# Loading batch zero's first keys in fp32 on SyncE, and its second softmax on two-bank tiles

## Chip, cores and metric

One core of a Trainium2 chip. The metric is the device time of one execution in microseconds (us), the median of several. On one core there is no second die to compare with.

## The reference, cut to what matters

```python
batch, n_heads, seq, head_dim = (8, 8, 576, 64);  n_pack = 32
def sm_attn(qq, kk, vv):                 # scale = 1/8
    s = scale * np.matmul(qq, kk.transpose(0, 1, 3, 2));  s = s - np.max(s, axis=-1, keepdims=True)
    a = np.exp(s);  a = a / (np.sum(a, axis=-1, keepdims=True) + 1e-09)
    return np.matmul(a, vv)
p_packed = sm_attn(p, k, v)              # 32 packed tokens a head look at 576 tokens
out = sm_attn(q, p_packed, p_packed)     # 576 tokens look at the 32
x = out.transpose(0, 2, 1, 3).reshape(8 * 576, 512)
h = x @ w_in                             # 512 -> 2048
y = (np.maximum(h, 0) ** 2) @ w_out      # 2048 -> 512
```

## The kernel before

The kernel merges the second attention and w_in: M = p_packed times w_in, then F1 = attention weights times M, squared, and F2 times w_out. Its steps for a batch: X (expand p into pT_bd), Tk and Tq (transposes of keys and queries on VectorE, DVE), S1 (p times keys), PV (times values), XT (pq_bd), M, S2 and N (second softmax), F1, F2. A planner simulates the engines while the program is built and so fixes the order of instructions on every engine; the durations in it are only its guesses.

All loads but the first p go through GpSimd's queue (POOL), which casts fp32 to bf16 on the way; I call it the casting queue.

```python
def dma_kq(self, name, qd):                      # one tile: 4 heads of keys or queries, 288 KB in bf16
    t = ... qkv.tile([P, JT * D], BF16, tag="kqb")
    nc.gpsimd.dma_start(t, src[self.b, qd * QH:(qd + 1) * QH].rearrange("h (a j) d -> (h a) (j d)", j=JT))
# [cut]
def ps_s(self, hf):                              # PSUM tile of the second softmax
    if hf is None:                               # whole tokens (all batches but 0): two banks, pool shared with F1
        ps = ps_h.tile([P, 2, 512], F32, name="ps_s", tag="h");  keep_clock(ps[:, 0, :256])
        return ps[:, :, :HALF]
    ps = ps_att.tile([P, 512], F32, name="ps_a", tag="a")   # batch 0, half of the tokens: one bank, shared with M
    keep_clock(ps[:, :256])                      # matmuls on zeros in a planned gap of TensorE
    return ps[:, :HALF].unsqueeze(1)
# [cut] order of the loads:
# p of batches 0, 1 (ACT queue) | k, k, v x4, q x2 of batch 0, w_in x2, q x2 (second halves), w_in x6, w_out x2,
# k, k, v x4, q, q of batch 1, w_out x6, k, k of batch 2, p of batches 2 to 7, v x4, q, q of batch 2, batch 3 ...
```

The softmax here doesn't subtract the row's maximum and nothing guards it: scores larger than these inputs give would overflow.

## Time and profile before

Median 252.97 us (252.92 to 253.29). The profiled execution spans 252.1 us; a second profile of the same kernel, taken later, spans 251.3 us, and the times of the timed runs belong to spans of about 251.3 us, so that the first profile is a slow one of its kind.

| what | before |
|---|---|
| TensorE (PE) busy from 60 to 250 us | 188.0 of 190 us |
| rate of the casting queue from 10 to 44 us | 202 GB/s landed (204 in the second profile) |
| first S1 / PV / S2 / F1 of batch 0 | 6.9 / 11.85 / 17.56 / 23.06 us |
| TensorE's waits from 23 to 66 us | 1.6 us |

From the page of the kernel before, three rows of 40 slices of 6.3 us: busy tenths of PE, mean busy tenths of the DMA engines, GB/s moved.

```profile
...
PE   4887989999999999999999999999999999999993
...
DMA  6999999999999972589111111110122013122233
GB/s 112 184 206 202 205 207 208 197 241 219 216 213 231 219 138 48 86 143 176 42 47 39 42 46 42 42 44 13 41 52 64 10 43 79 42 73 72 70 79 83
...
```

TensorE is nearly full from the seventh slice on, but the DMA engines are full from the second to the fourteenth, at 184 to 241 GB/s: work can't run ahead of its load. (TensorE's busy time up to 25 us is in good part clock-keeping matmuls: 11.8 us of them in this profile, none later.)

The chain that ended last, from its first 70 us: start, length, what.

```profile
...
3.02 6.76 DMA v_r<-in_v_dram
...
18.42 10.68 DMA k_b<-in_k_dram
...
29.38 8.45 DMA w_out_b<-in_moe_w_out_dram
...
38.12 11.37 DMA p_b<-in_p_dram
...
54.20 8.53 DMA v_r<-in_v_dram
...
```

It runs through one load after the other. The timeline (start, length, engine, line, operation, output and inputs, shapes, count; in brackets the idle time before and what ended it):

```profile
...
6.01 0.84 DVE L455 STREAM_TRANSPOSE kT<-k_b 128x320 f32<-128x320 f32 x2 [1.21 <-DMA k_b<-in_k_dram]
...
6.90 1.04 PE L466 MATMUL ps_a<-pT_bd,kT 128*128 128x128 bf16 x8 [3.32 <-DVE kT L455]
...
11.28 0.49 DVE L352 COPY v_b<-v_r 128x1280 bf16<-128x1280 bf16 x1 [3.04 <-DMA v_r<-in_v_dram]
...
11.85 0.28 PE L501 MATMUL ps_pp<-e,v_b 128*128 128x64 bf16 x4
...
15.05 0.61 PE L539 MATMUL ps_a<-w_in_b,pp 64*32 64x512 bf16 x8
...
17.56 0.65 PE L566 MATMUL ps_a<-qT,pq_bd 128*128 128x288 bf16 x4
...
23.06 1.14 PE L615 MATMUL ps_h<-a,M 128*128 128x288 bf16 x8
...
```

p has landed at 3.0 us. The keys land at 6.0, when DVE transposes the first, the last values at 11.15, when DVE casts v_b. M (L539, the 64x512 matmuls) comes before S2 (L566, ps_a), and both use the two one-bank tiles, so that S2 follows M's casts; F1 (L615) starts at 23.06 us.

The windows of the first microseconds; the last three columns are granted clock, DMA share and GB/s (this early, the 1.00 of the clock is no reading; see e13 and e14):

```profile
...
core 0: us, PE busy (x) PEld busy (x) DVE busy (x) ACT busy (x) POOL busy (x), PEclk, DMA share, GB/s
...
2.50:3.00 0.50, 0.50 (x5) 0.34 (x3) 0.27 (x1) 0.00 (x0) 0.50 (x1) 1.00 1.05 71
3.00:3.50 0.50, 0.50 (x3) 0.10 (x1) 0.46 (x2) 0.00 (x0) 0.50 (x2) 1.00 0.81 69
3.50:4.00 0.50, 0.09 (x1) 0.00 (x0) 0.45 (x3) 0.00 (x0) 0.50 (x2) 1.00 0.87 143
4.00:4.50 0.50, 0.00 (x0) 0.00 (x0) 0.47 (x3) 0.00 (x0) 0.50 (x2) 1.00 0.96 175
...
```

From 2.0 to 2.5 us, at 226 GB/s, p came in as fp32. The casting queue then starts at 70 GB/s and needs until about 4.5 us to reach its steady rate. The two longest groups of TensorE's waits from 23 to 66 us:

```profile
...
engine line waited for: us in total, times, longest us
PE ps_o L671 <- DMA w_out_b<-in_moe_w_out_dram: 0.7, 2, 0.5
PE ps_a L466 <- POOL pT_bd L352: 0.4, 1, 0.4
...
```

### The profile page before, as it was taken

Reading aid. Unit: us, or ns where it says so; the run is one execution under the profiler, and the core shown is the slowest. Engines: PE = TensorE matmul, PEld = TensorE weight load, DVE = VectorE, ACT = ScalarE, POOL = GpSimd, SP = SyncE. Lnnn points to the kernel's source line nnn. Section 1 sums busy time; section 2 is a strip of 40 time slices with the busy share of each in tenths; the row PEclk is TensorE's granted clock in tenths of the full one; section 3 lists DMA queues with packets and bytes.
Section 4 is the critical chain, followed back from the end, with each engine's and each line's share of the span. In section 5 each row is a group of like instructions: output and inputs, shape, how many; then the busy total and the mean of one; then the engine's idle time right before and its main releaser. Section 6 shows DMA issues by size and latency. Waiting matters only on the chain.

```text
span 252.1 us, 4976 instructions
## 1 busy us (share of the span) xinstructions
PE 239.6 (95%) x1935; PEld 143.6 (57%) x1935; DVE 143.5 (57%) x249; ACT 158.4 (63%) x275; POOL 61.7 (24%) x122
## 2 busy tenths in 40 slices
PE   4887989999999999999999999999999999999993
PEld 2765674466645666666456665665555655544453
DVE  5453968688988666895675858855146405400000
ACT  2448786678778777886687767777876853511110
POOL 7696465385655401150100000000000000000000
PEclk9999999999999999999999999999999999999999
DMA  6999999999999972589111111110122013122233
GB/s 112 184 206 202 205 207 208 197 241 219 216 213 231 219 138 48 86 143 176 42 47 39 42 46 42 42 44 13 41 52 64 10 43 79 42 73 72 70 79 83
DMA packets 27159, 28.44 MB, mean 113 GB/s; under 512 B 5760, under 2 KB 18816, under 8 KB 27136
## 3 DMA queue, kind: packets, MB, share of 16 engines
q0 software_dynamic: 19504, 18.55, 46.2%
q1 hardware_dynamic: 6912, 9.32, 13.8%
q10 hardware_dynamic: 720, 0.26, 0.4%
q8 instruction: 15, 0.25, 0.4%
q14 instruction: 8, 0.07, 0.1%
HBM read 37.22 MB, written 9.44 MB: 185 GB/s over the span
## 4 chain that ended last, share of the span: by engine, by line
PE 69%; DMA 20%; POOL 5%; SPq 1%; issue 1%; DVE 1%; ACT 1%; DVEq 0%; ACTq 0%; POOLq 0%
PE ps_o L671 40%; PE ps_h L605 19%; DMA v_r<-in_v_dram 6%; DMA p_b<-in_p_dram 5%; DMA k_b<-in_k_dram 4%; DMA w_out_b<-in_moe_w_out_dram 3%; PE ps_m L539 3%; PE ps_s L566 2%; DMA out_dram<-o_sb 2%; PE ps_a L466 2%; POOL w_in_b L428 2%; SPq L680 1%; PE ps_pp L501 1%; PE ps_s L578 1%; POOL v_r L420 1%
## 5 line engine op out<-in xcount | busy, mean ns | idle before, releaser
L671 PE MATMUL ps_o<-w_out_b,gT 128*128 128x512 bf16 x560 | 143.8, 379 | 1.0 <-DMA w_out_b<-in_moe_w_out_dram 0.7
L634 ACT ACTIVATE r<-ps_h 128x576 bf16<-128x576 f32 x112 | 70.9, 649 | 25.8 <-PE ps_h L605 22.4
L671 PEld LDWEIGHTS <-gT 128*128 128x128 bf16 x560 | 53.6, 98 | 47.6 <-issue 3.6
L605 PE MATMUL ps_h<-a,M 128*128 128x288 bf16 x448 | 71.1, 286 | 0.0
L641 DVE TENSOR_TENSOR gT<-r 128x1152 bf16<-128x1152 bf16 x64 | 47.0, 751 | 24.6 <-ACT r L634 14.3
L605 PEld LDWEIGHTS <-M 128*128 128x128 bf16 x448 | 43.6, 98 | 25.0
L352 DVE COPY o_sb<-ps_o 128x512 f32<-128x512 f32 (+1 forms) x19 | 12.8, 676 | 45.2 <-PE ps_o L651 27.6
L350 ACT COPY o_sb<-ps_o 128x512 f32<-128x512 f32 (+1 forms) x18 | 10.3, 575 | 31.3 <-DMA out_dram<-o_sb 23.0
L352 DVE CAST M<-ps_m 128x1024 bf16<-128x1024 f32 x14 | 17.1, 1224 | 11.6 <-PE ps_m L539 11.6
L449 DVE STREAM_TRANSPOSE qT<-q_b 128x1152 bf16<-128x1152 bf16 (+1 forms) x18 | 21.9, 1232 | 3.2 <-DMA q_b<-in_q_dram 3.1
L420 POOL DMA_DIRECT2D v_r<-in_v_dram x32 | 18.8, 592 | 9.4 <-DVE v_b L352 3.3
L350 ACT CAST M<-ps_m 128x1024 bf16<-128x1024 f32 x14 | 14.2, 1012 | 6.5 <-PE ps_m L539 6.4
L592 DVE SCALAR_TENSOR_TENSOR a<-e,rD,ls 128x576 bf16<-128x576 bf16 (+1 forms) x18 | 13.1, 745 | 4.5 <-ACT ls L586 4.3
L473 ACT ACTIVATE e<-ps_a 128x512 bf16<-128x512 f32 x16 | 8.8, 597 | 9.9 <-PE ps_a L466 9.8
L455 DVE STREAM_TRANSPOSE kT<-k_b 128x320 f32<-128x320 f32 (+1 forms) x32 | 12.9, 449 | 1.8 <-DMA k_b<-in_k_dram 1.8
L352 POOL COPY pT_bd<-pT 32x128 bf16<-32x128 bf16 x28 | 10.0, 358 | 13.9 <-PE ps_a L480 12.4
L573 ACT ACTIVATE e<-ps_s,rD 128x576 bf16<-128x576 f32 x14 | 9.7, 738 | 5.3 <-PE ps_s L566 5.3
L466 PE MATMUL ps_a<-pT_bd,kT 128*128 128x128 bf16 x128 | 9.5, 231 | 3.7 <-DVE kT L455 3.3
L408 POOL DMA_DIRECT2D k_b<-in_k_dram x16 | 8.7, 544 | 15.9 <-DVE kT L455 6.5
L374 PE MATMUL ps_a<-idle_b 128*128 128x256 bf16 x59 | 9.1, 306 | 3.2 <-ACT e L573 1.4
L466 PEld LDWEIGHTS <-kT 128*128 128x128 bf16 x128 | 8.5, 103 | 6.0 <-DVE kT L455 4.0
L374 PEld LDWEIGHTS <-idle_b 128*128 128x128 bf16 x79 | 8.3, 107 | 6.4 <-issue 3.9
(65 smaller groups left out, 197.9 us busy)
## 6 DMA issues: line engine op xcount, KB each, us to landing
out_dram<-o_sb SPq DMA_DIRECT2D x140, 64.0 KB, 1.7
k_b<-in_k_dram POOLq DMA_DIRECT2D x16, 288.0 KB, 8.8
q_b<-in_q_dram POOLq DMA_DIRECT2D x14, 288.0 KB, 8.9
v_r<-in_v_dram POOLq DMA_DIRECT2D x16, 160.0 KB, 8.6
v_r<-in_v_dram POOLq DMA_DIRECT2D x16, 128.0 KB, 8.5
w_in_b<-in_moe_w_in_dram POOLq DMA_DIRECT2D x8, 256.0 KB, 7.7
w_out_b<-in_moe_w_out_dram POOLq DMA_DIRECT2D x8, 256.0 KB, 9.3
q_b<-in_q_dram POOLq DMA_DIRECT2D x4, 144.0 KB, 6.9
```

What stands on the lines that cost most here:

```text
L350: nc.scalar.copy(dst, src)
L352: eng.tensor_copy(dst, src)
L374: nc.tensor.matmul(ps, lhsT=idle_b[:, :P], rhs=idle_b, start=True, stop=True)
L420: nc.gpsimd.dma_start(self.vr[32 * i:32 * i + 32, h0:h1, :n * D], src[:, :, J0[i] * D:(J0[i] + n) * D])
L449: nc.vector.transpose(self.qT[:, qd, :, j0 * 32:j1 * 32].rearrange("p dh (j a) -> p j dh a", a=32), self.t.qb[qd][:, j0 * D:j1 * D].rearra ...
L455: nc.vector.transpose(self.kT[:, qd, :n * P].rearrange("p (g jp a) -> p jp g a", jp=4, a=32)[:, i:i + 2], self.t.kb[qd][:, J0[i] * D:(J0[i ...
L466: nc.tensor.matmul(ps[:, g * P:(g + 1) * P], lhsT=self.kT[:, qd, g * P:(g + 1) * P].bitcast(BF16).rearrange("p (t two) -> p two t", two=2) ...
L592: nc.vector.scalar_tensor_tensor(out=self.a2[:, qd, n0:n1].rearrange("p (c n) -> p c n", n=HALF), in0=self.e2[qd, hf], scalar=self.rD[:, q ...
L605: nc.tensor.matmul(ps[:, c, :HALF], lhsT=a.M[:, qd, fb * FB:(fb + 1) * FB], rhs=a.a2[:, qd, c * HALF:(c + 1) * HALF], start=(qd == 0), sto ...
L634: nc.scalar.activation(dst, src, ACT.Relu)
L641: eng.tensor_tensor(out=gT[:, fb - 1:fb + 1, o:o + S], in0=r, in1=r, op=ALU.mult)
L671: nc.tensor.matmul(po[t], lhsT=gT[:, fb, n0:n0 + P], rhs=w_out_b[:, fb, :], start=(fb == 0), stop=(fb == NFB - 1))
```

## The change

Its intent: key tile 0 of batch 0 is the first thing that the kernel needs. SyncE can load it at once as fp32, in parallel with GpSimd's issues, and ScalarE and VectorE each cast a half. One load less is then in the casting queue. And batch 0's second softmax needs no longer wait for M's tiles. Cut to its core (left out are the planner's durations of other steps, changed by up to 0.08 us, and its start times of the engines, changed by 0.2 to 0.4 us):

```diff
+            def dma_k_f32(self, qd):
+                self.kf = stg.tile([P, JT * D], F32, name="k_f", tag="kf")
+                nc.sync.dma_start(self.kf, k[self.b, qd * QH:(qd + 1) * QH].rearrange(...))
+                self.kb[qd] = qkv.tile([P, JT * D], BF16, name="k_b", tag="kqb")
+            def cast_k(self, qd, i, eng):
+                w = JH * D
+                cast(eng, self.kb[qd][:, i * w:(i + 1) * w], self.kf[:, i * w:(i + 1) * w])
             def ps_s(self, hf):
-                if hf is None:
+                if hf is None or self.b in SPLIT:
                     ps = ps_h.tile([P, 2, 512], F32, name="ps_s", tag="h")
-                    return ps[:, :, :HALF]
+                    return ps[:, :2 if hf is None else 1, :HALF]
-                return [kq("k", 0), kq("k", 1)] + vv(0, 1) + [ ...
+                return [kq("k", 1)] + vv(0, 1) + [ ...
-            return [res[0], res[2], res[1], res[4], res[3], res[6], res[5], res[7]]
+            return [res[0], res[2], res[1], res[3], res[4], res[6], res[5], res[7]]   # S2, S2, N, N of the first halves
+        plan.stream(0, [Step("Lk.0.0", [stage([("SP", 0.45, lambda: L[0].dma_k_f32(0))]), ...
+        plan.stream(5, [Step("Ck.0.0", ...   # the halves on ACT or DVE
```

More of the change, by code (lines that the diff above doesn't have):

```diff
@@ L24 @@
 BDW = 384
+SPLIT = (0,)
 INF = float("inf")
@@ L408, in dma_kq @@
                 nc.gpsimd.dma_start(t, src[self.b, qd * QH:(qd + 1) * QH].rearrange("h (a j) d -> (h a) (j d)", j=JT))
+            def dma_k_f32(self, qd):
+                self.kf = stg.tile([P, JT * D], F32, name="k_f", tag="kf")
+                nc.sync.dma_start(self.kf, k[self.b, qd * QH:(qd + 1) * QH].rearrange("h (a j) d -> (h a) (j d)", j=JT))
+                self.kb[qd] = qkv.tile([P, JT * D], BF16, name="k_b", tag="kqb")
+            def cast_k(self, qd, i, eng):
+                w = JH * D
+                cast(eng, self.kb[qd][:, i * w:(i + 1) * w], self.kf[:, i * w:(i + 1) * w])
             def dma_q_half(self, qd, hf):
@@ L715, in load_steps @@
             if b in SPLIT:
-                return [kq("k", 0), kq("k", 1)] + vv(0, 1) + [
+                return [kq("k", 1)] + vv(0, 1) + [
                     load_step(f"Lq.{b}.{qd}.{hf}", 0.56, 0.78, lambda qd=qd, hf=hf: L[b].dma_q_half(qd, hf), [("kqb", 1)] if hf == 0 else [])
@@ L741, in tr_steps @@
             if nm == "q" and b in SPLIT:
-                return [Step(f"Tq.{b}.{qd}.{hf}", [stage([("DVE", 0.71, lambda qd=qd, hf=hf: T[b].tr_q(qd, hf))])],
+                return [Step(f"Tq.{b}.{qd}.{hf}", [stage([("DVE", 0.78, lambda qd=qd, hf=hf: T[b].tr_q(qd, hf))])],
                              [f"Lq.{b}.{qd}.{hf}"] + old, (), [("kqb", 0, f"Lq.{b}.{qd}.0")] if hf else []) for hf in range(2) for qd in QDS]
             return [Step(f"T{nm}.{b}.{qd}", [stage([("DVE", us, lambda qd=qd: (T[b].tr_k if nm == "k" else T[b].tr_q)(qd))])],
-                         [f"L{nm}.{b}.{qd}"] + old, (), [("kqb", 0, f"L{nm}.{b}.{qd}")]) for qd in QDS]
+                         [f"Ck.0.0" if (nm, b, qd) == ("k", 0, 0) else f"L{nm}.{b}.{qd}"] + old, (),
+                         [("kqb", 0, f"L{nm}.{b}.{qd}")]) for qd in QDS]
         def s1_steps(b):
@@ L773, in m_steps @@
                              [stage([("PE", 0.66, lambda c=c: T[b].m(c))]),
-                              stage(*[[("ACT", 1.05, lambda c=c, e=e: T[b].m_out(c, e, A)),
-                                       ("DVE", 1.15, lambda c=c, e=e: T[b].m_out(c, e, V))] for e in QDS])],
+                              stage(*[[("ACT", 1.01, lambda c=c, e=e: T[b].m_out(c, e, A)),
+                                       ("DVE", 1.23, lambda c=c, e=e: T[b].m_out(c, e, V))] for e in QDS])],
                              [f"XT.{b}/1.0"] + [f"LWI.{2 * c + j}.{i}" for i in range(2) for j in range(2)], [("h", 2)], [("h", 1, None)])
@@ L790, in s2_steps @@
             wide = b in WIDE
-            pool, m = ("h", 2) if wide else ("a", 1)
+            pool, m = "h" if wide or b in SPLIT else "a", 2 if wide else 1
             for qd, hf in halves(b):
@@ L801, in s2_steps @@
                                  stage([("ACT", 0.65 if wide else 0.43, lambda qd=qd, hf=hf: T[b].n_inv(qd, hf))]),
-                                 stage([("DVE", 0.75 if wide else 0.46, lambda qd=qd, hf=hf: T[b].n_mul(qd, hf))])],
+                                 stage([("DVE", 0.82 if wide else 0.52, lambda qd=qd, hf=hf: T[b].n_mul(qd, hf))])],
                                 [f"S2.{b}.{qd}.{hf}"], [(pool, 1), ("ls", 1)],
@@ L897, in kernel_impl @@
         NB_ACTQ = -1
-        SPLIT = (0,)
         WIDE = tuple(b for b in range(B) if b not in SPLIT)
@@ L902, in kernel_impl @@
         setup()
-        plan.base.update(DVE=2.5, POOL=0.8, ACT=0.5, SP=0.3, DMA=1.2, PE=3.6)
+        plan.base.update(DVE=2.7, POOL=1.2, ACT=0.75, SP=0.7, DMA=1.2, PE=3.6)
         plan.stream(0, [pload(0, 2)])
@@ L908, in kernel_impl @@
         plan.stream(0, ld)
+        plan.stream(0, [Step("Lk.0.0", [stage([("SP", 0.45, lambda: L[0].dma_k_f32(0))]), stage([("-", 0.75, lambda: None)]),
+                                        stage([("DMA", 1.5, lambda: None)])], (), [("kqb", 1)], (), lag=0.7)])
+        plan.stream(5, [Step("Ck.0.0", [stage([("-", 0.0, lambda: None)]),
+                                        stage(*[[("ACT", 0.67, lambda i=i: L[0].cast_k(0, i, A)),
+                                                 ("DVE", 0.45, lambda i=i: L[0].cast_k(0, i, V))] for i in range(2)])], ["Lk.0.0"])])
         plan.stream(0.5, [Step("Z", [stage([("POOL", 2.6, setup_rest)])], ["Lq.0.1.1/1.0"])])
```

## The prediction

> **What bounds the kernel now (252.97 us).** In the table of windows PE is busy 188.0 of 190 us from 60 to 250 us at full clock: that stretch is TensorE-bound and the change does not touch it. The first 23 us are start-up (PE busy 15.9 us, about 11 of it clock-keeping matmuls on idle_b). Between 29 and 65 us PE waits only about 1.6 us, 0.7 of it for w_out. Yet the chain of waits up to 63 us consists mainly of loads (v, k of batch 1, w_out 29.4-37.8, p 38.1-49.5, v 54.2-62.8), and the loads run at a constant 205 GB/s landed from 4 to 50 us: work is gated by the place of its load in a full queue.
>
> Start-up of batch 0 (timeline): p lands 3.0, keys 6.0 and 7.4, values 9.0 to 11.25; PV 11.8; pq_bd done 14.7. M's first chunk (15.1) holds both one-bank tiles until its casts end at 16.8, so S2 starts at 17.5; its four halves finish their first token half at 21.7; F1 starts at 23.06.
>
> **What the change does.**
> 1. Keys of heads 0-3 leave the POOL queue: one 0.6 us issue less there and one 295 KB landed transfer less, about 1.4 us (key tile to key tile). Instead a 590 KB fp32 load starts on SyncE at 0.8-1.2 us. The windows show the DMA engines empty before 1.9 us and moving 70 GB/s from 2.5 to 3.5 us, so most of it should fit into unused time. The Trainium skill ("DMA: Bandwidth & Descriptors", SWDGE vs HWDGE) says that a cast during DMA needs GpSimd, hence the casts.
> 2. Two half casts are added, estimated 0.45-0.6 us on DVE (from 0.29 us for 256 columns) and 0.65 on ACT, in parallel: keys ready at about 5.2. Alone this is off the critical path: PV waits for the values.
> 3. Batch 0's second softmax goes to the two-bank pool, idle until F1, so S2 need not follow M's casts: S2 at 13.5-15, and with first halves in front F1 at 18.5-20, then limited by w_in.
> 4. Other diffs are planner costs; they may reorder slightly.
>
> **How much reaches the time.** Values should land at 9.6-10 (1.3-1.6 us earlier), and the queue behind moves as much. The 4 us by which F1 starts earlier can't all be kept: F2 needs the last w_out chunks (landing 38 to 44 us now), batch 1 its queries (35-37), and those move only with the queue. PE will run dry around 28-37 us, where it is full now. I expect the queue's shift, 1.3-1.6 us, plus a few tenths from existing waits: about 2 us.
>
> Predicted 251.0 us, 8 in 10 between 249.5 and 252.3. Faster by over 2%: 0.04; within 2%: 0.94; slower by over 2%: 0.02.
>
> **What would show each step.** k_f landed by 4.7; last v landing at 9.6-10; S2 before 15 and F1 before 20; PE waits between 26 and 40 us rising by 1-3 us, for w_out, k or q; PE busy after 65 us unchanged; last w_out landing 1-2 us earlier.
>
> **What would make it wrong.** p and k_f start together: p may land later, and DVE has p's cast, transpose and expansion (1.7 us), a half cast and key transposes in line, so keys may gain nothing. The fp32 load may take its bandwidth from key tile 1 and the values: no queue shift, under 1 us. In the other direction, if tensor work rather than loads binds at 38-45 us, the early F1 could give 3-4 us.

## The result, and the profile after

Median 252.5 us (252.28 to 253.21), against 253.1 us for the kernel before in the same rounds: ratio 0.9981, 95% interval 0.9960 to 1.0003. In five more rounds (run e2 below) the ratio was 0.9974, 0.9956 to 0.9993. Ratios are the mean time of one kernel's runs over that of the other's of the same rounds, so not quite the ratio of the medians. The gain is thus about 0.5 us; I had predicted 2 us, and 252.5 lies 0.2 us above the range. The two profiles differ by 1.6 us (252.1 and 250.5), but 0.8 us of that is the slow profile of before, see e1. The first interval still holds no gain at all; that of e2 does not.

From the page after, the same rows:

```profile
...
PE   4699989989999999999999999999999999999994
...
DMA  7999999999999974595111111110112022122233
GB/s 169 190 206 204 203 206 209 207 227 221 221 220 227 223 112 94 83 196 100 42 45 42 42 43 39 49 32 14 49 46 61 18 52 76 42 73 72 71 80 84
...
```

The chain after, first 66 us:

```profile
...
3.06 7.38 DMA v_r<-in_v_dram
...
18.47 9.46 DMA k_b<-in_k_dram
...
28.21 8.24 DMA w_out_b<-in_moe_w_out_dram
...
36.74 11.33 DMA p_b<-in_p_dram
...
50.20 0.72 POOL pT_bd L353
...
```

The loads of batch 1, w_out and p are still in it, 1.2 to 1.4 us earlier than in the first, slow profile of before (k of batch 1 lands at 27.93 us, p at 48.07), but only 0.2 to 0.3 us earlier than in its second profile (28.11 and 48.34 us). The timeline after (line numbers are about ten higher; S1 L476, M L549, S2 L576, F1 L625):

```profile
...
0.73 0.39 SPq L413 DMA_DIRECT2D k_f<-in_k_dram  x1
0.76 0.46 ACTq L385 DMA_DIRECT2D p_f<-in_p_dram  x1
...
4.47 0.67 ACT L351 CAST k_b<-k_f 128x576 bf16<-128x576 f32 x1 [2.46 <-DMA k_f<-in_k_dram]
4.82 0.29 DVE L353 CAST p_b<-p_f 128x256 bf16<-128x256 f32 x1 [2.06 <-DMA p_f<-in_p_dram]
...
8.03 1.89 PE L476 MATMUL ps_a<-pT_bd,kT 128*128 128x128 bf16 x16 [4.24 <-DVE kT L465]
...
11.34 0.49 DVE L353 COPY v_b<-v_r 128x1280 bf16<-128x1280 bf16 x1 [2.65 <-DMA v_r<-in_v_dram]
...
12.08 0.28 PE L511 MATMUL ps_pp<-e,v_b 128*128 128x64 bf16 x4
...
15.14 0.65 PE L576 MATMUL ps_s<-qT,pq_bd 128*128 128x288 bf16 x4
...
15.72 0.41 PE L549 MATMUL ps_a<-w_in_b,pp 64*32 64x512 bf16 x8
...
20.86 0.65 PE L625 MATMUL ps_h<-a,M 128*128 128x288 bf16 x4
...
```

Four things are to be seen. k_f lands before 4.5 us, as predicted. p, issued 0.03 us after it, lands at 4.8 us instead of 3.0, so that S1 starts 1.1 us later than before, not earlier: VectorE has p's cast, transpose and expansion in front of its half of the keys, which it casts only at 6.6 us. The values are cast at 11.34 us, as before, not at 9.6 to 10. And S2 now precedes M, 2.4 us earlier than before, and F1 starts at 20.86, 2.2 us earlier. The windows after:

```profile
...
2.50:3.00 0.50, 0.50 (x5) 0.34 (x3) 0.27 (x1) 0.00 (x0) 0.50 (x1) 1.00 1.01 406
3.00:3.50 0.50, 0.50 (x4) 0.24 (x2) 0.00 (x0) 0.00 (x0) 0.50 (x2) 1.00 0.98 379
3.50:4.00 0.50, 0.29 (x2) 0.00 (x0) 0.00 (x0) 0.00 (x0) 0.50 (x2) 1.00 1.00 274
4.00:4.50 0.50, 0.00 (x0) 0.00 (x0) 0.00 (x0) 0.03 (x1) 0.50 (x2) 1.00 1.19 241
5.00:6.00 1.00, 0.00 (x0) 0.00 (x0) 0.92 (x4) 0.14 (x1) 1.00 (x2) 1.00 1.00 133
...
```

k_f moves at 380 to 406 GB/s (p joins in the last part), but in this time the casting queue moves nothing: its first packet is at 4.03 us, at 2.61 in the kernel before, though GpSimd issued its first load at 1.23 us in both. Its start-up loss is there again, in another form: in its first microsecond it moves 175 KB (78 in the kernel before), in the second 130 KB (170 before). After three microseconds that is 479 against 443 KB; in the second profiles of the two kernels, 416 against 433 KB (added up from the packet records). TensorE's two longest groups of waits from 23 to 66 us, after:

```profile
...
PE ps_a L476 <- POOL pT_bd L353: 0.9, 1, 0.9
PE ps_o L681 <- DMA w_out_b<-in_moe_w_out_dram: 0.7, 1, 0.7
...
```

### The profile page after: what moved, and what is told of

The parts are those of the page before. It is cut to its first block, busy times and chain, and to the rows that moved or that the text cites. A ratio compares the mean times of both kernels' runs of the same rounds, so it can differ in the third digit from the quotient of the medians.

```text
span 250.5 us, 4939 instructions
## 1 busy us (share of the span) xinstructions
PE 236.1 (94%) x1898; PEld 143.0 (57%) x1928; DVE 146.8 (59%) x254; ACT 156.1 (62%) x272; POOL 60.4 (24%) x121
## 4 chain that ended last, share of the span: by engine, by line
PE 67%; DMA 20%; POOL 4%; SPq 4%; ACT 2%; issue 2%; DVE 0%; ACTq 0%; POOLq 0%
PE ps_o L681 34%; PE ps_h L615 21%; DMA out_dram<-o_sb 5%; DMA p_b<-in_p_dram 5%; DMA k_b<-in_k_dram 4%; SPq L690 4%; DMA w_out_b<-in_moe_w_out_dram 3%; DMA v_r<-in_v_dram 3%; PE ps_m L549 3%; PE ps_s L576 2%; PE ps_a L476 2%; ACT o_sb L351 2%; POOL w_in_b L438 2%; PE ps_pp L511 2%; PE ps_s L588 1%
## 5 line engine op out<-in xcount | busy, mean ns | idle before, releaser
L681 PE MATMUL ps_o<-w_out_b,gT 128*128 128x512 bf16 x530 | 138.3, 379 | 2.2 <-DMA w_out_b<-in_moe_w_out_dram 0.7
L353 DVE COPY o_sb<-ps_o 128x512 f32<-128x512 f32 (+1 forms) x20 | 13.5, 675 | 49.7 <-PE ps_o L661 27.6
L583 ACT ACTIVATE e<-ps_s,rD 128x576 bf16<-128x576 f32 (+1 forms) x18 | 11.8, 685 | 8.0 <-PE ps_s L576 7.9
L476 PE MATMUL ps_a<-pT_bd,kT 128*128 128x128 bf16 x128 | 9.4, 231 | 5.3 <-DVE kT L465 4.2
L409 POOL DMA_DIRECT2D q_b<-in_q_dram x14 | 7.8, 555 | 20.0 <-DVE qT L459 13.9
L476 PEld LDWEIGHTS <-kT 128*128 128x128 bf16 x128 | 8.5, 104 | 7.0 <-DVE kT L465 4.7
L353 POOL COPY pT_bd<-pT 32x128 bf16<-32x128 bf16 x28 | 9.4, 335 | 10.1 <-PE ps_a L490 8.6
L593 ACT ACTIVATE ls<-ps_s 128x576 f32<-128x576 f32 (+1 forms) x18 | 10.6, 599 | 0.8 <-PE ps_s L588 0.5
```

Source lines behind the costliest of these rows:

```text
L353: eng.tensor_copy(dst, src)
L476: nc.tensor.matmul(ps[:, g * P:(g + 1) * P], lhsT=self.kT[:, qd, g * P:(g + 1) * P].bitcast(BF16).rearrange("p (t two) -> p two t", two=2) ...
L681: nc.tensor.matmul(po[t], lhsT=gT[:, fb, n0:n0 + P], rhs=w_out_b[:, fb, :], start=(fb == 0), stop=(fb == NFB - 1))
```

## Experiments

**Theory A:** up to about 60 us the casting queue sets the time; a shift of it is worth its size; the fp32 load takes back at its head (later start) what it saves behind. **Rival B**, in several forms: the time hangs on the start-up chain of batch 0 (keys, S1, PV, S2, F1), or the queue's shift is absorbed later. This table sums up what the traces and timings show. "First" is the first packet of the casting queue. "1.16 MB" is when the queue had landed 1.16 MB beyond what it carries of key tile 0, nearly all of key tile 1, the values and the first query halves of batch 0; I added it up from the trace's packet records. The last columns are starts. All are from one profile each, in us; ratio and interval are from all timed runs. The profiled execution was the slowest of its runs in e3, e6 and e11 and the fastest in after, e2, e4, e8 and e14, so a row's starts and its ratio do not belong to the same execution.

```
run                          first  v landed  1.16 MB   S1     PV     F1     ratio (95%)
before                        2.61   11.15    11.02    6.90  11.85  23.06
e1  before again              2.61   10.38    10.98    6.82  12.09  22.80   1.0001 (0.9989-1.0013)
after                         4.03   11.22    10.63    8.03  12.08  20.86   0.9981 (0.9960-1.0003)
e2  after again               3.90   11.17    10.98    8.03  12.80  21.88   0.9974 (0.9956-0.9993)
e3  keys only                 3.83   11.44    11.38    7.80  13.36  25.94   0.9993 (0.9974-1.0011)
e4  softmax only              2.60   11.30    11.13    7.00  12.98  21.62   0.9989 (0.9966-1.0011)
e5  no key load               2.60    8.91     9.63    6.36  10.18  19.16   0.9935 (0.9902-0.9967)
e6  keys, then p              3.87   11.43    10.93    7.45  12.24  21.39   0.9964 (0.9939-0.9989)
e7  after + p split           4.00   12.38    11.26    8.03  13.56  23.11   1.0090 (1.0063-1.0117)
e8  softmax only + p split    2.60   10.81    11.12    6.79  13.07  22.32   1.0080 (1.0052-1.0109)
e9  p, then keys              3.43   10.18    10.63    8.68  13.34  22.38   0.9979 (0.9954-1.0003)
e10 half of the keys          3.24   11.55    11.54    6.82  14.08  23.44   1.0015 (0.9989-1.0041)
e11 no key load, old softmax  2.60    9.25     9.75    5.68  10.96  23.11   0.9945 (0.9923-0.9966)
e12 p split, mended           3.85   11.12    11.15    8.03  12.81  22.26   1.0025 (0.9997-1.0054)
e13 few fills                 4.02   10.71    10.96    8.03  11.38  21.25   0.9992 (0.9970-1.0013)
e14 p, then keys, few fills   3.25   10.24    10.85    8.81  11.77  21.04   0.9980 (0.9952-1.0007)
```

### e1 and e2: both kernels again

No edit.

> The kernel before, unchanged, as a control. A: the profiled before (span 252.1 us) was slow for its kind, its timed runs correspond to about 251.3 us; so this profile should span about 251.3 us and the ratio be 1.000 within 0.002. B: the 1.6 us between the two profiles (252.1 and 250.5) is the true gain and the timed medians understate it; then this profile spans 252 us again.

> The changed kernel, unchanged, with more rounds. A (gain equals the shift of the load queue, 0.45 us in the two profiles at 2 to 8 MB landed): ratio 0.998, span about 250.7 us. B (gain equals the difference of the two profiles, 1.6 us): ratio 0.994.

Measured: 253.07 us, ratio 1.0001, span of the profile 251.3 us: the control holds, and the first profile of before was 0.8 us slow. The changed kernel: 252.49 us, ratio 0.9974. Its profile spans 250.0 us, less than expected. The timed result is between A's 0.998 and B's 0.994, near A, and its interval leaves out 0.994; so single profiles can't be subtracted from one another here.

### e3 and e4: each part alone

e3 keeps the key load and puts the softmax back, e4 the other way round:

```diff
# e3
-                if hf is None or self.b in SPLIT:
+                if hf is None:
-            pool, m = "h" if wide or b in SPLIT else "a", 2 if wide else 1
+            pool, m = ("h", 2) if wide else ("a", 1)
-            return [res[0], res[2], res[1], res[3], res[4], res[6], res[5], res[7]]
+            return [res[0], res[2], res[1], res[4], res[3], res[6], res[5], res[7]]
# e4
-                return [kq("k", 1)] + vv(0, 1) + [
+                return [kq("k", 0), kq("k", 1)] + vv(0, 1) + [
-        plan.stream(0, [Step("Lk.0.0", ...      # and Ck.0.0; Tk.0.0 waits for the load again
```

> Only the fp32 key load and its casts; batch 0's second softmax back on the one-bank tiles in the old order. A (loads bind until 60 us, the gain is the queue's shift): the whole gain stays, ratio 0.998, although the first tensor work of F1 is back at about 22.5 us. B (the earlier F1, 20.9 instead of 23.1 us, makes the gain): no gain or a loss, ratio 1.000 or more, because v still lands at 11.2 us.

> Only the second softmax on the two-bank tiles with first halves in front; keys loaded as before. A (queue's shift): F1 starts at about 21 us, but ratio 1.000. B (earlier F1 makes the gain): ratio 0.998 or lower, as good as the whole change.

Measured: 0.9993 and 0.9989. The key load alone gives nothing that the rounds can tell from zero, where my theory had expected the whole gain (0.998): in the profiled execution, the slowest of the six, the queue isn't earlier at all (1.16 MB at 11.38 us), so the premise failed there, and not only the size; but the interval still holds 0.998. The softmax alone gives nothing certain either, though its F1 starts at 21.62 us. And e3's F1 starts at 25.94 us, 3.1 us later than in e1, while this execution took only 0.6 us longer than e1's (253.67 and 253.07 us): where F1 starts is not what the time hangs on. e3 is not quite the old order, though: in e3, and in e11 below, the planner put M behind the second softmax (M at 23.6 and 20.8 us, at 15.05 in the kernel before). Which part makes the 0.25% of the whole change these two don't settle; the parts' intervals hold 0 and 0.25%.

### e5 and e11: the key load taken away

Key tile 0 of batch 0 is zeros (meant to be wrong; the comparison with the reference passed all the same). e5 has the new softmax, e11 the old one with e3's edit.

```diff
-                self.kf = stg.tile([P, JT * D], F32, name="k_f", tag="kf")
-                nc.sync.dma_start(self.kf, k[...])
                 self.kb[qd] = qkv.tile([P, JT * D], BF16, name="k_b", tag="kqb")
+                nc.vector.memset(self.kb[qd], 0.0)
-                # casts and their step
```

> The whole change, but the fp32 key load and its casts are gone and key tile 0 of batch 0 is filled with zeros by VectorE (wrong result on purpose). A (the fp32 load takes back, at the head of the queue, what it saves behind): without it the cast loads start at 2.6 us again, key tile 1 lands at about 6.0, v's last part at 9.8 and the whole queue is about 1.4 us earlier than in the kernel before; the time falls by 1.0 to 1.6 us, ratio 0.994 to 0.996. B (a shift of the queue is absorbed later, for instance at the load of p for batches 2 to 7): the landings are 1.4 us earlier but the ratio stays at 0.997 to 0.999.

> No load of key tile 0 (zeros, wrong on purpose), and the second softmax of batch 0 as in the kernel before. A (a shift of the load queue is worth its size by itself): ratio 0.9945 to 0.996, within 0.002 of the run with the new softmax (0.9935). B (the shift pays only together with the earlier F1): ratio 0.998 or more.

Measured: 251.01 us, ratio 0.9935, and 251.84 us, ratio 0.9945. The casting queue starts at 2.60 us again, and is about 1.3 us earlier at its head (1.16 MB at 9.63 and 9.75 us, 11.0 before) and 0.8 to 1.4 us at 8 MB (43.57 and 43.86 us, 44.93 and 44.68 in the two profiles of before). From e5's timeline:

```profile
...
6.36 1.91 PE L475 MATMUL ps_a<-pT_bd,kT 128*128 128x128 bf16 x16 [2.13 <-DVE pT_bd L353]
...
9.03 0.49 DVE L353 COPY v_b<-v_r 128x1280 bf16<-128x1280 bf16 x1 [1.86 <-DMA v_r<-in_v_dram]
...
10.18 0.42 PE L510 MATMUL ps_pp<-e,v_b 128*128 128x64 bf16 x4
...
```

v_b is cast at 9.03 us, even earlier than the 9.6 to 10 that I had predicted for the change itself. In e11, F1 starts as late as in the kernel before:

```profile
...
23.11 1.15 PE L624 MATMUL ps_h<-a,M 128*128 128x288 bf16 x8
...
```

So about 1.3 us of queue are worth 1.4 to 1.65 us of time (0.55 to 0.65% of 253 us; the intervals go from 0.8 to 2.5 us), with or without an earlier F1: A. The rival, that a shift is absorbed later, falls. The scatter between executions points the same way: over the 13 profiles in which p is not split, the moment at which the queue had landed 8 MB goes with the time of that same execution (correlation 0.69). And the change would have had this gain if its load had cost nothing: the difference of e2 and e5, about 1 us (give or take nearly as much), is what the fp32 load, with its casts, takes back.

### e6 and e9: p ahead of the keys

```diff
# e6
-                nc.sync.dma_start(self.kf, k[...])
+                nc.scalar.dma_start(self.kf, k[...])
# e9: the same, and issued right behind p
-                return Step("LP.0", [stage([("ACTQ", 0.5, lambda: load_p(b0, b1, A))])], ...
+                return Step("LP.0", [stage([("ACTQ", 0.5, lambda: (load_p(b0, b1, A), L[0].dma_k_f32(0)))])], ...
```

> The whole change with the fp32 key load issued on ScalarE's queue behind p, instead of on SyncE beside it. Both theories: p lands at about 3.0 us instead of 4.8, S1 starts before 7.5 instead of 8.0. A: PV still waits for v (11.2 to 11.9 us) and the ratio is that of the whole change, 0.997 to 0.998. B (p's late landing is what cost the gain): PV before 11 us and ratio 0.995 or lower.

> As the run with p first, in which the planner had put p second after all; now p is issued first and the fp32 keys second, both on ScalarE's queue. Both theories: p lands at about 3.0 us, keys at about 4.9, S1 starts before 7.6 us. A (values and the cast loads bind): cast loads still start only at about 3.9 us, PV near 12 us, ratio 0.997 to 0.998 as the whole change. B (p's late landing cost the gain): PV before 11 us and ratio 0.995 or lower.

e6 missed its purpose: the planner put the keys first and p second, and p landed at 4.65 us. Its ratio, 0.9964, is still within what the whole change shows. e9 has the order right: p lands at 3.07 us. But the keys land at 7.06 us, not at 4.9, because now the casting queue starts at 3.43 us and shares the engines with the rest of them; S1 starts at 8.68 us. Ratio 0.9979, as the whole change. So p early with the keys late brings no more; p and keys both early was not run. e9 shows something else:

```profile
...
10.30 0.49 DVE L353 COPY v_b<-v_r 128x1280 bf16<-128x1280 bf16 x1 [0.96 <-DMA v_r<-in_v_dram]
...
11.26 2.29 PE L375 MATMUL ps_pp<-idle_b 128*128 128x256 bf16 x10 [0.26 <-ACT e L483]
...
13.34 0.42 PE L511 MATMUL ps_pp<-e,v_b 128*128 128x64 bf16 x4
...
```

The values are cast at 10.30 us and S1's last result is out at about 11.5 us, but PV starts at 13.34 us behind ten clock-keeping matmuls, planned for a gap that was not there. So "PV waits for the values", as A had it, isn't true of this run, and PV had not yet been moved by itself. That is the reason for e13 and e14.

### e10: half of the keys

```diff
-                self.kf = stg.tile([P, JT * D], F32, name="k_f", tag="kf")          # 590 KB
+                self.kf = stg.tile([P, w], F32, name="k_f", tag="kf")               # 295 KB, w = JH * D
+                # the other half: nc.gpsimd.dma_start(self.kb[qd][:, w:], k[...][:, w:]), first in the casting queue
```

> Only half of key tile 0 comes as fp32 on SyncE, the other half by the casting queue. A (every byte that SyncE reads at the head delays the start of the cast loads by as much as it saves behind them): the cast loads start at about 3.3 us, between 2.6 and 3.9, the bytes that the queue has landed at 11 us, less what it no longer carries, are as before within 0.3 us, ratio 0.997 to 0.999. B (the fp32 load only fills idle engines and something else slows the cast loads): they start at 2.6 or at 3.9 regardless of the size.

Measured: the casting queue starts at 3.24 us, between 2.6 and 3.9 as A says. Three sizes of SyncE's load (0, 295, 590 KB) give 2.60, 3.24 and 3.8 to 4.03 us: each half moves the start by 0.6 to 0.8 us, about what its bytes take at 400 GB/s (0.74 us, an estimate from the rate above). The queue at 1.16 MB is 0.5 us later than before, more than A's 0.3, and the ratio, 1.0015, is above the 0.997 to 0.999 that I expected, a miss, though its interval (from 0.9989) just reaches that range: this version is no better than the kernel before.

### e7, e8 and e12: p of batches 2 to 7 in two parts

The chain runs through the load of p, so a smaller load there should show the queue's worth once more.

```diff
-            ld += load_steps(b)[:2] + ([pload(2, B)] if b == 2 else []) + load_steps(b)[2:]
+            ld += load_steps(b)[:2] + ([pload(2, 4)] if b == 2 else [pload(4, B)] if b == 4 else []) + load_steps(b)[2:]
# e12: the second part at b == 3, its transpose to wait for S1 of batch 3
```

> The whole change, with p of batches 2 to 7 loaded in two parts, batches 4 to 7 only with batch 4. A (the load queue binds until about 60 us and the chain of waits runs through the p load, landing at 47 to 48 us in the changed kernel): the queue is about 1 us shorter at 50 us, p of batches 2 and 3 lands about 1 us earlier, and the ratio is 0.993 to 0.995. B (TensorE binds by then): ratio as the whole change, 0.997 to 0.998.

> Second softmax changed, keys loaded as before, p split as in the run before. A (the key load is worth nothing): the same ratio as with the key load, within 0.001. B (the key load is worth its part): 0.001 to 0.002 slower than that.

> The whole change with p of batches 2 and 3 loaded before batch 2's values and p of batches 4 to 7 before batch 3's, its transpose ordered behind S1 of batch 3, so that VectorE can't block on it as it did in the two runs with p split at batch 4. A (the queue binds up to about 60 us): the wait of TensorE for the expansion of p near 50 us is gone, ratio 0.994 to 0.996. B (the queue is only as binding as its end, which is not earlier): 0.997 to 0.998.

Measured: 1.0090, 1.0080 and 1.0025. e7 and e8 are my mistake. In e7's timeline,

```profile
...
69.04 0.45 DVE L393 STREAM_TRANSPOSE pT<-p_b 128x256 f32<-128x256 f32 x1 [3.19 <-DMA p_b<-in_p_dram]
...
71.00 0.39 PE L681 MATMUL ps_o<-w_out_b,gT 128*128 128x512 bf16 x1 [1.79 <-DVE gT L651]
```

VectorE stands 3.2 us at the transpose of the second part of p, whose load lands at 69.0 us, later than the planner thought, and TensorE waits behind it for gT. They test neither theory, except that e8 (0.0010 faster than e7) again gives the key load no worth. In e12 that block is gone, and so is TensorE's wait for pT_bd near 50 us (p's first part lands at 47.06 us), but the time isn't better than before: 1.0025, where A had 0.994 to 0.996 and B 0.997 to 0.998, a miss for both. An earlier p at 47 us did not pay here. Its profile has TensorE busy 11.1 of the 12 us from 66 to 78 us, where e2 has 11.9; what of its new order does that I have not found out.

### e13 and e14: few clock-keeping matmuls in front of PV

```diff
                     self.ps_pp = ps_att.tile([P, 512], F32, name="ps_pp", tag="a")
+                    plan.fill = min(plan.fill, 2)
                     keep_clock(self.ps_pp[:, :256])
```

e13 is the whole change with it, e14 is e9 with it.

> The whole change with at most two clock-keeping matmuls in front of PV of batch 0 (10 before). Both theories: PV starts when v_b is cast, at about 11.9 us, instead of 12.1 to 12.8. A (the load queue alone sets the time): F1 earlier by up to 1 us, ratio unchanged at 0.997 to 0.998. B (the start-up chain through PV counts as well): ratio 0.993 to 0.995. If TensorE runs slow after the missing matmuls (417 instead of 273 ns a matmul), PV and S2 get longer and F1 gains nothing.

> p first and keys second on ScalarE's queue (as in the mended run, whose v landed at 10.2 us but whose PV started only at 13.3 us behind ten clock-keeping matmuls), and at most two of those matmuls. Both: PV at about 11.4 us. A: ratio still 0.997 to 0.998. B: 0.993 to 0.995.

Measured: PV at 11.38 and 11.77 us, 1.4 and 1.6 us earlier than in e2 and e9, F1 0.6 and 1.3 us earlier. In e13, PV now does wait for the values:

```profile
...
11.38 0.39 PE L512 MATMUL ps_pp<-e,v_b 128*128 128x64 bf16 x4 [0.19 <-DVE v_b L353]
...
```

The ratios are 0.9992 and 0.9980, no better than e2 and e9 without it: A. The start-up chain of batch 0, earlier by about a microsecond, gives nothing that the rounds show. The shift itself is less sure: against the first profile of after, e13's PV is only 0.7 us earlier, and its F1 (21.25 us) 0.4 us later.

Part of such differences goes with TensorE's clock. Careful: the trace's records of it begin with its first change, in most profiles only at 10.6 to 15.9 us (after 11.43, e2 13.87, e3 15.65), and a 1.00 before that is no reading. In e8, e9 and e13 the records begin near 4 us, with 3.4 us at full clock and then 6.83 us at half; that is why their mean is about 0.985 where others show 1.0. In e9's windows (granted clock third from the right):

```profile
...
0.00:10.00 10.00, 4.06 (x25) 2.97 (x26) 5.23 (x20) 2.20 (x3) 7.02 (x16) 0.87 0.94 177
10.00:14.00 4.00, 3.74 (x33) 2.96 (x31) 1.98 (x3) 2.37 (x4) 3.73 (x11) 0.50 1.18 178
...
```

Others seem to have been slow there too, unrecorded: the clock-keeping matmuls in front of PV take 417 ns each (median) in e2, before its first record, and 280 ns in the first profile of after, whose record begins among them. So PV and F1, 0.7 and 1.0 us later in e2 than in after, probably came later in part by the clock; yet e2's execution was the shorter one (250.0 against 250.5 us). And e3's two shortest spans (250.5 and 250.4 us, the others 251.2 to 251.9) are the two with a mean clock of 0.985. So no run shows the clock to be where the gain went. The Trainium skill ("TensorE: Matmul & The Clock Gate", What's actually happening) says that the clock falls to half after an idle window of about 3.4 us and that the window runs free of the kernel's start, so that runs differ. e9 and e13 agree: TensorE did nothing from 4.08 to 7.49 us and from 3.92 to 7.33 us, 3.41 us each, and the clock was halved at the end of both; but in e8 it was halved at 7.81 us although TensorE had been busy for 0.95 of the 3.42 us before.

## Why the prediction was wrong

- **What bounds the kernel: right.** Loads gate the time to about 60 us, TensorE after. e5 and e11 show it: about 1.3 us of queue made 1.4 to 1.65 us of time, in e11 with F1 where it was. e12 is the exception that I can't explain.
- **The step that failed: "Values should land at 9.6-10 (1.3-1.6 us earlier), and the queue behind moves as much."** The values landed at 11.2 us. Over all nine profiles with the full fp32 load the queue had landed its 1.16 MB at 10.97 us on average (10.63 to 11.38), over the four with the cast load at 11.06 us (10.98 to 11.13): a shift of 0.1 us in place of 1.3 to 1.6. At 8 MB it is the same 0.1 us (44.78 and 44.86 us, over the profiles in which p is not split). The term under it was "most of it should fit into unused time". I had read 70 GB/s as unused time, but from 1.87 to 2.65 us p was moving, and from 2.5 to 3.5 us the DMA share was already 1.05 and 0.81. The 590 KB, from 1.76 to 4.04 us at up to 406 GB/s, took p's place (p's first packet went from 1.87 to 3.15 us) and pushed the casting queue's first packet back by 1.4 us (2.61 to 4.03), just what one 295 KB transfer less saves at 205 GB/s (1.44 us, an estimate). The casting queue's start-up loss came again behind them: it was not a hole at a fixed place, but went along with the queue. Why the casting queue moved no packet beside k_f, while p did, the traces don't show.
- **The warnings were right.** "p may land later ... keys may gain nothing": p landed 1.8 us later and S1 started 1.1 us later. That seems to have cost nothing: in e14, S1 starts later still, at 8.81 us, and PV at 11.77 us all the same, as early as in the kernel before. The other warning, "the fp32 load may take its bandwidth from key tile 1 and the values: no queue shift, under 1 us", is what happened, with the number. I had given it too little weight in the range.
- **S2 ahead of M: right in kind, too large in size, and worth little.** S2 came at 15.14 to 16.15 us (13.5 to 15 predicted), F1 at 20.9 to 21.9 us (18.5 to 20 predicted), because pq_bd, which S2 needs, was no earlier (its first copy starts at 13.66 us, at 13.67 before). That "the 4 us by which F1 starts earlier can't all be kept" was right: in e3 F1 starts 3 us later, in e13 0.6 us earlier than in e2, and the ratios can't be told apart.
- **"PE will run dry around 28-37 us": not so.** In the windows TensorE is busy 10.0 of the 11 us from 29 to 40 us before, and 9.85 of them after, 0.2 us less instead of 1 to 3 (10.48 and 10.41 in the second profiles). Its longest wait in the first profile after is for pT_bd near 50 us (0.9 us), the expansion of p behind the load of p; in e2 that wait is gone, so it is not a fixed cost of the change.
- **Open.** The 0.5 us that the change does gain can't be put down to one part: keys alone 0.07%, softmax alone 0.11%, both with intervals of 0.2% to either side.

## What to carry to other kernels

Moving a load to another queue hardly shifted the first queue here, since the DMA engines under both queues had no time to spare when it ran; 70 GB/s beside a DMA share near 1 was not spare time. Before counting it as saved, look at when the other queue's first packet would then start: measure it, and take the load away altogether to see what the most could be (here about 1.65 us, of which the load itself took back about 1.0). When an early stage moves by 2 us and the time does not, look for the resource that the later stages are fed from, here the place in the load queue.

## What the Trainium skill lacked or had wrong

- "DMA: Bandwidth & Descriptors", Queues, rings and completion order, says that each DMA engine goes round the queue rows for which it has work, at packet granularity. In the first microseconds here this was not to be seen: with k_f under way the casting queue, issued at 1.23 us, moved nothing until 4.03 us, and p, issued 0.03 us behind k_f on another queue, had its first packet at 3.15 us. With p in front and k_f second (e9) the casting queue and k_f did share, from 3.43 us to 6.6 us, k_f with the smaller part after 4 us (27 to 64 against 82 to 179 GB/s). Which of the two one gets the page doesn't say; nor do the traces show whether the casting queue had its work ready before 4 us.
- The same page, Issuing engines are not separate DMA queues, says that issuing from several engines will "only save the time on the sequencer it takes to initiate the DMA". The runs agree: with the full fp32 load the queue is 0.1 us earlier on average, less than the 0.6 us of the issue.
- The same page, Specifications, gives a first-byte latency of about 0.6 us for SyncE and ScalarE and about 1 us for GpSimd. From the start of the issue to the first packet it was 1.03 us for k_f (0.73 to 1.76) and 1.37 us for the first cast load (1.24 to 2.61); from the end of the issuing instruction (1.12 and 1.84 us) 0.64 and 0.77 us. That a row of cast loads then needs two more microseconds to reach its steady rate (70 to 198 GB/s landed in the kernel before) I found on no page; in the changed kernel, behind k_f, it began at 142 GB/s and dipped to 112 at 5.5 us.
- That a cast during DMA needs GpSimd (SWDGE vs HWDGE on that page), on which the prediction rests for the casts, no run here tests.
